# Order of the first loads, clears and splits, identity products ahead of the first keys, and key differences formed behind the first lower half, in a gated mix of two attentions

## The chip, the core and the metric

The kernel runs on one core of one Trainium2 chip. A core has five engines that work in parallel, each on its own list of instructions in a fixed order: TensorE (PE in the profile, with its weight loads as PEld) for matrix products into PSUM, VectorE (DVE), ScalarE (ACT), GpSimd (POOL), and SyncE (SP), which here only starts DMA transfers. ACT and POOL start transfers too. An engine waits for another through semaphores; the instruction that waits holds up all that stands behind it on its engine. The metric is the device time of one execution in microseconds (us), lower is better; each time is the median of several runs, and one further execution of each kernel is profiled.

## The reference

Two attentions read the same x (2048 rows of 512), and a gate mixes their outputs. Branch A is a local attention of 32 heads over 8 keys, two rows apart; branch B has 32 query heads and one head of keys and values, over all 2048 keys.

```python
def _A_ref(x, wqkv, wo):                      # H = 32, Dh = 16, W = 8, dil = 2
    q, k, v = qkv[0], qkv[1], qkv[2]          # of x @ wqkv
    idx = pos[:, None] - off[None, :]         # off = arange(8) * 2
    logits = einsum("bhsd,bhswd->bhsw", q, k[idx]) * scale
    attn = softmax(where(idx >= 0, logits, -1e9))
    return einsum("bhsw,bhswd->bhsd", attn, v[idx]) @ wo

def _B_ref(x, wq, wk, wv, wo):
    q = (x @ wq), 32 heads of 16;  k = x @ wk;  v = x @ wv
    p = softmax(einsum("bhqd,bkd->bhqk", q, k) * Dh ** -0.5)
    return einsum("bhqk,bkd->bhqd", p, v) @ wo

g = sigmoid((x * gate_w).sum(-1))
return g * a + (1 - g) * b
```

## The kernel before, in words

The program has four stages. All numbers of lines are those of the profile before.

**Opening.** x arrives transposed in four blocks t of 512 rows, each in four pieces c of 128 x 512 (`xraw[t, c]`, 256 KB each); `wkr` holds the key weights, `wqr[0..3]` the raw query weights (256 KB each). SP starts the sixteen x pieces (L114), ACT `wkr` (L150) and the four query weights (L117). A value is carried as a high and a low part: ACT rounds the high part (L81), DVE or POOL subtracts it to get the low part (L82); this is `split`, with `split_x` for x and `split_wq` for the query weights. PE forms the keys of block t from `xraw` and `wkr` (`keys(t)`, L189, four products over 128 rows); ACT and DVE write them into `kst` (L193, L194). `first_query(m)` forms the queries of the first row block for column groups 0 and 1 (L826, twelve products); they go out to a scratch tensor `qd` (L206), and `stack(u)` reads them back as the stacked tile `qst` of unit u (L283, L284). Rows 32 to 63 and 96 to 127 of each `qst` tile are cleared once (`clear`, L159), the halo of branch A's scratch tensor `ad` is written with zeros (L819, L820), the right half of `vst` with ones (L821).

**Front stream** (`front_stream`). PE runs the remaining query products and branch A's projections (L1002). These 78 lumps of twelve steps are split over the two halves of the PE array: the lower half takes the first 64 rows of the contraction, the upper half the last 64, and both add into one PSUM bank, so that a lower and an upper product can run at the same time. Between them stand products of queries with keys (L315) whose maxima DVE takes (L349): these are the running maxima that softmax needs for each unit. A cheaper form takes two key blocks at once: `kd` holds differences of keys, formed by `half_keys` (four products with `sel`, L365, over the full 128 rows) and `half_parts` (ACT L373, DVE L377); then a product with `kd` (L386), a relu on ACT (L396), a product with the keys (L315) and one DVE instruction (L406) give the maximum over two blocks. `queries_post` empties the PSUM bank of a finished query lump with two ACT copies (`qraw`, L217, of which there is a single buffer, and `qhi`, L218); POOL subtracts `qlo` (L225) from them, and SP writes both out.

**Exponentials.** For 512 steps PE forms scores (L454), ACT exponentials (L456), PE weighted sums (L465), with the remaining maxima (L315, L337, L349) and the output rows (L709) between them, while POOL works through branch A. **Tail**: the last four output rows.

What sets the order: the host code keeps three clocks (`clk`, for PE, ACT and DVE), one time for each PSUM bank at which it is expected to be free (`free`), and lists of tasks with due times. `front_stream` walks two positions, one per half of the array, and at each point writes down the step that its clocks say is ready. The clocks choose the order only; on the chip the engines follow that order at their own pace. The upper half may start a lump only behind a step of ACT or DVE that the plan expects to be finished (`behind`, `after_upper`). `wanted` says that the key differences are still to be formed: before, `half_keys` is written down as soon as both `pd` banks are expected to be free (29.0 on the plan's clocks, with the stream started at 26.5).

Of the kernel before, what the change touches and what calls it, by code (L numbers as in the profile page):

```python
# [6 lines left out]
F32 = mybir.dt.float32  # L7
# [41 lines left out]
def gated_mix_kernel(ctx, tc, xt, wa, wk, wq, wo_a, wo_b, out):  # L49
# [36 lines left out]
    def after(eng, ready, dur):  # L86
        clk[eng] = max(clk[eng], ready) + dur
        return clk[eng]
# [23 lines left out]
    def load_x(t):  # L112
        for c in range(C):
            nc.sync.dma_start(xraw[t, c], xt[:, t, c, :])  # L114

    def load_wq(cc):
        nc.scalar.dma_start(wqr[cc], wq[:, cc])  # L117
# [5 lines left out]
    def split_x(t, eng):  # L123
        for c in range(C):
            split(xh[t][c // 2][:, c % 2, :], xl[:, t, c, :], xraw[t, c], eng)
# [25 lines left out]
    for cc in range(4):  # L151
        load_wq(cc)
    for t in range(NQB):
        load_x(t)
    make_identity(nc, ident)

    def clear(k, eng):
        for b in (0, 64):
            eng.memset(qst[k][b + 32:b + 64].bitcast(F32), 0.0)  # L159

    for k in range(3):
        clear(k, nc.vector)

# [127 lines left out]
    free = {"m1": 0.0, "e0": 0.0, "e1": 0.0, "po": 0.0, "d0": 29.0, "d1": 29.0}  # L291
# [66 lines left out]
    wanted = [0]  # L358

    def half_keys():  # L360

        clk["pe"] = max(clk["pe"], free["d0"], free["d1"])
        for y in range(2):
            for g in range(2):
                nc.tensor.matmul(ds[g], sel[:, y], kst[:, (2 * g + y) * 512:(2 * g + y + 1) * 512], start=(y == 0), stop=(y == 1))  # L365
        clk["pe"] += 1.0
        free["d0"] = free["d1"] = clk["pe"] + 4.0
        tasks.append((clk["pe"] + 0.3, half_parts, (ups[0],)))

    def half_parts(up):  # L370
        kd.append(cp.tile([P, 2, 512], F32R, name="kd", tag="kd", bufs=1))
        for g in range(2):
            got = nc.scalar.activation(kd[0][:, g], ds[g], AF.Identity, scale=mk[:, 0:1])  # L373
            at = after("act", clk["pe"], 0.65)
            mark(got, at, up)
        for g in range(2):
            nc.vector.scalar_tensor_tensor(kd[0][:, g], ds[g], mk[:, 1:2], kd[0][:, g].bitcast(F32), op0=ALU.mult, op1=ALU.add)  # L377
            free[f"d{g}"] = after("dve", at + 0.1, 0.7) + 0.1
            formed.add(g)

# [434 lines left out]
    split_wq(0)  # L815
    for k in range(3, NB):
        clear(k, nc.gpsimd)
    zero = wp.tile([NAG, HALO * AN], F32, name="zero", tag="aext", bufs=2)
    nc.gpsimd.memset(zero, 0.0)  # L819
    nc.gpsimd.dma_start(ad[:, 0:HALO, :].rearrange("g r n -> g (r n)"), zero)  # L820
    nc.gpsimd.memset(vst[:, :, 16:32], 1.0)  # L821
# [24 lines left out]
    split_x(0, nc.vector)  # L846
# [8 lines left out]
    post_k()  # L855
    post_k = keys(2)
    post_q = first_query(1, fb[2])
    post_k()
    post_q()
# [6 lines left out]
    clk.update(pe=26.5, act=26.5, dve=26.5)  # L866
    stacked[:] = [0.0] * 2 + [30.0] * 2
    post_k()
    fill_one(m1, "m1")
    fill_one(po, "po")  # L870
    split_x(3, nc.gpsimd)
# [186 lines left out]
    def pick(b):  # L1058
# [11 lines left out]
        if not (ended and any(todo)) and (mine or slots and fillable() and not (paired() and not ended) and len(half) < 8) and (b or told[0] or mine):  # L1070
            for dst, key in ((m2[:, 0, :], "m2"),) if eb else zip(ds, ("d0", "d1")) if ended else ((m1, "m1"), (po, "po")):
                if fits(key):
                    return lambda dst=dst, key=key: fill_odd(b, dst, key)
# [4 lines left out]
    def front_stream(seq):  # L1078
# [4 lines left out]
        while told[0] < len(seq):  # L1083
            if wanted and max(free["d0"], free["d1"]) <= max(cl) + 0.05:
                wanted.clear()
                half_keys()
                cl = [clk["pe"]] * 2
                continue
# [172 lines left out]
```

## Time and profile before

| what | value |
|---|---|
| median of three runs | 1503.94 us (1502.19 to 1504.04) |
| the profiled execution | 1504.74 us, of which the span from first to last instruction is 1503.0 us |
| PE, DVE, ACT, POOL busy | 1481.7, 1198.1, 1251.3, 944.5 us |
| mean granted TensorE clock | 0.997 of full speed |
| first product of the keys | 5.29 us |
| first product of the front stream | 27.79 us |
| first lump products on both halves at once | 37.76 us |

A busy PE says only that some product was running. A product that covers 64 of the 128 rows leaves the other half of the array free, and two such products can overlap; a row such as "0.95 PE ... x2" is such a pair. The two stages to look at are the opening and the first 15 us of the front stream; the rest of the kernel runs on after them in an order that the same plan makes.

### The profile page before, as it was taken

To read this page: it belongs to the slowest core of one execution; us is meant where nothing else is said; L and a number is where in the kernel's file an instruction comes from. 1 tells how busy PE (TensorE), PEld (TensorE's weight loads), DVE (VectorE), ACT (ScalarE), POOL (GpSimd) and SP (SyncE) were. 2 spreads that over 40 slices of the span, in tenths; PEclk is the share of its full clock that TensorE was granted. 3 is DMA by queue.
4 is the path that set the end of the run, shared out by engine and by line. 5 is a ranking of instruction groups with operands and counts; after the bars stand their busy time and mean duration, and the time that the engine had idled before them with its cause. 6 is when DMAs were issued, how large, how long until landed. Compare 5 with 4: busy or idle time off the path is not lost.

```text
span 1503.0 us, 29096 instructions
## 1 busy us (share of the span) xinstructions
PE 1481.7 (99%) x10945; PEld 730.0 (49%) x10945; DVE 1198.1 (80%) x1789; ACT 1251.3 (83%) x1591; POOL 944.5 (63%) x1667
## 2 busy tenths in 40 slices
PE   8999999999999999999999999999999999999998
PEld 4899999633333333333333373333333733373334
DVE  5777878778888888888888888888888888888821
ACT  4787988699999999999999939999999489939994
POOL 7331898887979888888889787887840401151000
PEclk9999999999999999999999999999999999999999
DMA  6553342320211210211202111121100000000000
GB/s 219 144 162 114 116 144 80 97 77 12 77 51 38 86 38 31 77 48 41 77 13 69 45 59 46 41 69 41 41 12 12 23 19 2 1 23 8 1 2 29
DMA packets 43909, 85.64 MB, mean 57 GB/s; under 512 B 9520, under 2 KB 25960, under 8 KB 39672
## 3 DMA queue, kind: packets, MB, share of 16 engines
q1 hardware_dynamic: 36200, 44.00, 9.7%
q0 software_dynamic: 6560, 37.95, 7.8%
q8 instruction: 86, 1.41, 0.4%
q10 hardware_dynamic: 1008, 1.84, 0.3%
q14 instruction: 55, 0.45, 0.1%
HBM read 57.97 MB, written 25.25 MB: 55 GB/s over the span
## 4 chain that ended last, share of the span: by engine, by line
PE 93%; DVE 3%; ACT 1%; issue 1%; DMA 1%; DVEq 0%; ACTq 0%
PE po L465 32%; PE pe L454 25%; PE pf L1002 11%; PE pm L315 8%; PE ps L315 5%; PE pe L709 5%; PE pd L386 2%; DVE mx L337 1%; PE po L315 1%; PE pf L189 1%; DVE mx L349 1%; DVE tt L479 1%; PE pe L1192 1%; DMA ad<-stage 0%; ACT pexp L456 0%
## 5 line engine op out<-in xcount | busy, mean ns | idle before, releaser
L456 ACT ACTIVATE pexp<-pe 128x1024 f32<-128x1024 f32 x1024 | 991.1, 1022 | 94.3 <-PE pe L454 91.5
L337 DVE TENSOR_REDUCE mx<-pm 128x2 f32<-128x1024 f32 x525 | 641.0, 1221 | 165.7 <-PE pm L315 158.0
L454 PE MATMUL pe<-qst,kst 64*128 64x512 f32 x2048 | 566.9, 455 | 2.6 <-ACT pexp L456 1.2
L465 PE MATMUL po<-pexp,vst 128*32 128x512 f32 x4096 | 545.5, 605 | 3.4 <-DVE tt L479 2.3
L454 PEld LDWEIGHTS pe<-qst,kst 64*128 64x128 f32 x2048 | 233.7, 184 | 450.4 <-ACT pexp L456 442.2
L349 DVE TENSOR_REDUCE mx<-ps 128x1 f32<-128x512 f32 x476 | 323.9, 681 | 8.3 <-PE ps L315 7.3
L315 PE MATMUL ps<-kst,qst 62*128 62x512 f32 x602 | 252.4, 419 | 1.1 <-DVE mx L349 1.1
L315 PE MATMUL pm<-kst,qst 62*128 62x512 f32 x1054 | 222.7, 404 | 0.8 <-DVE mx L337 0.6
L527 POOL TENSOR_TENSOR pr<-aext 128x256 f32<-128x256 f32 x256 | 181.8, 737 | 4.8 <-PE pd L386 4.6
L587 POOL TENSOR_TENSOR oa<-oa,av 128x256 f32<-128x256 f32 x224 | 164.0, 732 | 15.7
L396 ACT ACTIVATE dd<-pd 128x512 f32<-128x512 f32 x252 | 147.6, 603 | 30.7 <-DVE mx L406 16.5
L465 PEld LDWEIGHTS po<-pexp,vst 128*32 128x32 f32 x4096 | 80.6, 108 | 179.8 <-issue 166.1
L315 PEld LDWEIGHTS ps<-kst,qst 62*128 62x128 f32 x602 | 111.2, 185 | 78.9 <-DVE mx L349 74.4
L584 POOL TENSOR_TENSOR av<-aext,lg 128x256 f32<-128x256 f32 x224 | 139.2, 622 | 13.6
L491 POOL TENSOR_TENSOR rl<-rl,gate_t 128x16 f32<-128x16 f32 x31 | 6.9, 221 | 190.5 <-DVE rl L485 190.4
L1002 PE MATMUL pf<-wah,xl 64*128 64x384 f32 (+1 forms) x496 | 121.1, 339 | 0.0
L1002 PE MATMUL pf<-wal,xh 64*128 64x384 f32 (+1 forms) x496 | 118.8, 338 | 0.0
L1002 PE MATMUL pf<-wah,xh 64*128 64x384 f32 (+1 forms) x496 | 117.2, 338 | 0.0
L406 DVE CUSTOM_DVE_ANT_0 dd<-po,dd 128x512 f32<-128x512 f32 x126 | 87.0, 691 | 31.8 <-PE po L315 17.8
L315 PEld LDWEIGHTS pm<-kst,qst 62*128 62x128 f32 x1054 | 103.4, 187 | 11.8 <-DVE mx L337 8.8
L406 DVE CUSTOM_DVE_ANT_0 dd<-ps,dd 128x512 f32<-128x512 f32 x126 | 87.0, 690 | 19.4 <-PE ps L315 5.6
L386 PE MATMUL pd<-kd,qst 62*128 62x512 f32 x252 | 100.8, 405 | 1.1 <-ACT dd L396 1.0
(188 smaller groups left out, 1610.6 us busy)
## 6 DMA issues: line engine op xcount, KB each, us to landing
aext<-ad POOLq DMA_DIRECT2D x32, 1056.0 KB, 5.6
ad<-stage SPq DMA_DIRECT2D x32, 384.0 KB
qst<-qd SPq DMA_DIRECT2D x64, 128.0 KB
xraw<-xt SPq DMA_DIRECT2D x16, 256.0 KB
qd<-qhi SPq DMA_DIRECT2D x16, 256.0 KB
qd<-qlo SPq DMA_DIRECT2D x16, 256.0 KB
qst<-qd SPq DMA_DIRECT2D x64, 64.0 KB
qst<-ml SPq DMA_DIRECT2D x228, 2.0 KB
```

Of the source, the lines that this page charges most:

```text
L315: nc.tensor.matmul(dst, qst[place(v)][b:b + 62, pr, t * P:(t + 1) * P], kst[b:b + 62, kc * 512:(kc + 1) * 512], start=True, stop=True)
L337: got = nc.vector.tensor_reduce(m[:, :, pr, t, kc], dst, AX.X, ALU.max)
L349: got = nc.vector.tensor_reduce(m[:, odd, pr, t, kc:kc + 1], dst, AX.X, ALU.max)
L396: got = nc.scalar.activation(dd[:, b], ds[b], AF.Relu)
L406: got = nc.vector.tensor_tensor_reduce(dd[:, b], dst, dd[:, b], 1.0, -FMAX, ALU.add, ALU.max, m[:, b, pr, t, kc:kc + 1])
L454: nc.tensor.matmul(bank[:, odd, :], kst[b:b + 64, kt * P:(kt + 1) * P], qst[place(u)][b:b + 64, pr, :], start=True, stop=True)
L456: got = nc.scalar.activation(e, bank, AF.Exp, scale=SCALE)
L465: nc.tensor.matmul(po[32 * i:32 * i + 32, :], vst[:, kt, :], pexp[s, i // 2][:, i % 2, :], start=(kt == 0), stop=(kt == NJ - 1))
L527: nc.gpsimd.tensor_mul(pr[:, k], q, e[:, o:o + NH, AC:2 * AC])
L584: nc.gpsimd.tensor_mul(av, e[:, o:o + NH, 2 * AC:].rearrange("p j (h d) -> p j h d", d=DH), lg[:, w].unsqueeze(3).to_broadcast([P, NH, AG, ...
L587: nc.gpsimd.tensor_add(ao, ao, av)
L1002: inst = nc.tensor.matmul(home(x)[0][:, :n], l[h], r[h], start=(i == 0 and b == 0), stop=(i == 3 * C - 1 and b == 1))
```

## The change

The diff touches the opening and the plan of the front stream.

- **Loads.** `wq` pieces 1 to 3 move from ACT's queue to SP's, each behind the x block of the same number; ACT starts `wkr` and `wq` piece 0 alone.
- **Clears.** DVE no longer clears three `qst` tiles first. POOL clears tiles 0 and 1 and writes the ones of `vst`; DVE clears tiles 2 and 3 between the posts of the keys; POOL clears tiles 4 to 8 as tasks of the front stream. The zeros of `ad` are written behind the third x block's low parts. The splits of the fourth x block are tasks too, one per piece.
- **Splits.** x piece 0 is split ahead of the first query weights.
- **Identity products.** Ten products of `ident` with itself (128 x 128, F32) stand ahead of the first keys; nothing reads what they write.
- **Last keys.** The first two products for maxima are written down ahead of the post of the last keys, so their DVE instructions stand ahead of it.
- **Key differences.** `half_keys` waits until the lower half has done the twelve steps of its first lump; the two ACT steps follow it at once, and the two DVE steps come when the plan's clock has passed them.
- **Plan.** The stream's clocks start at 24.6 in place of 26.5, the `pd` banks at 24.0 in place of 29.0; a half product for a maximum is taken by the lower half only once the upper half has done a step.

```diff
     def load_wq(cc):
-        nc.scalar.dma_start(wqr[cc], wq[:, cc])
+        (nc.sync if cc else nc.scalar).dma_start(wqr[cc], wq[:, cc])
...
-    def split_x(t, eng):
-        for c in range(C):
+    def split_x(t, eng, cs=range(C)):
+        for c in cs:
             split(xh[t][c // 2][:, c % 2, :], xl[:, t, c, :], xraw[t, c], eng)
...
     nc.scalar.dma_start(wkr, wk)
-    for cc in range(4):
-        load_wq(cc)
+    load_wq(0)
     for t in range(NQB):
         load_x(t)
+        if t:
+            load_wq(t)
     make_identity(nc, ident)
+    for k in range(10):
+        nc.tensor.matmul(m1[:, 0:P], ident, ident, start=True, stop=True)
...
-    for k in range(3):
-        clear(k, nc.vector)
-
+    for k in range(2):
+        clear(k, nc.gpsimd)
+    nc.gpsimd.memset(vst[:, :, 16:32], 1.0)
...
-    free = {"m1": 0.0, "e0": 0.0, "e1": 0.0, "po": 0.0, "d0": 29.0, "d1": 29.0}
+    free = {"m1": 0.0, "e0": 0.0, "e1": 0.0, "po": 0.0, "d0": 24.0, "d1": 24.0}
...
-    wanted = [0]
+    wanted = [0.0]
 
     def half_keys():
 
-        clk["pe"] = max(clk["pe"], free["d0"], free["d1"])
         for y in range(2):
             for g in range(2):
                 nc.tensor.matmul(ds[g], sel[:, y], kst[:, (2 * g + y) * 512:(2 * g + y + 1) * 512], start=(y == 0), stop=(y == 1))
         clk["pe"] += 1.0
-        free["d0"] = free["d1"] = clk["pe"] + 4.0
-        tasks.append((clk["pe"] + 0.3, half_parts, (ups[0],)))
-
-    def half_parts(up):
         kd.append(cp.tile([P, 2, 512], F32R, name="kd", tag="kd", bufs=1))
         for g in range(2):
             got = nc.scalar.activation(kd[0][:, g], ds[g], AF.Identity, scale=mk[:, 0:1])
-            at = after("act", clk["pe"], 0.65)
-            mark(got, at, up)
+            mark(got, after("act", clk["pe"] + T_LAT, 0.65))
+            free[f"d{g}"] = clk["act"] + 5.0
+        wanted[:] = [clk["act"] - 0.6]
+
+    def half_parts():
         for g in range(2):
             nc.vector.scalar_tensor_tensor(kd[0][:, g], ds[g], mk[:, 1:2], kd[0][:, g].bitcast(F32), op0=ALU.mult, op1=ALU.add)
-            free[f"d{g}"] = after("dve", at + 0.1, 0.7) + 0.1
+            free[f"d{g}"] = after("dve", free[f"d{g}"] - 5.0, 0.7) + 0.1
             formed.add(g)
+        wanted.clear()
...
     lumps = []
-    split_wq(0)
-    for k in range(3, NB):
-        clear(k, nc.gpsimd)
-    zero = wp.tile([NAG, HALO * AN], F32, name="zero", tag="aext", bufs=2)
-    nc.gpsimd.memset(zero, 0.0)
-    nc.gpsimd.dma_start(ad[:, 0:HALO, :].rearrange("g r n -> g (r n)"), zero)
-    nc.gpsimd.memset(vst[:, :, 16:32], 1.0)
...
-    split_x(0, nc.vector)
+    split_x(0, nc.vector, [0])
+    split_wq(0)
+    split_x(0, nc.vector, range(1, C))
     post_k()
...
     post_k()
+    clear(2, nc.vector)
     post_k = keys(2)
     post_q = first_query(1, fb[2])
     post_k()
+    clear(3, nc.vector)
     post_q()
...
     post_k = keys(3)
-    clk.update(pe=26.5, act=26.5, dve=26.5)
+    clk.update(pe=24.6, act=24.6, dve=24.6)
     stacked[:] = [0.0] * 2 + [30.0] * 2
-    post_k()
     fill_one(m1, "m1")
     fill_one(po, "po")
-    split_x(3, nc.gpsimd)
+    post_k()
+    for e in ("act", "dve"):
+        after(e, 0, 0.8)
+    zero = wp.tile([NAG, HALO * AN], F32, name="zero", tag="aext", bufs=2)
+    nc.gpsimd.memset(zero, 0.0)
+    nc.gpsimd.dma_start(ad[:, 0:HALO, :].rearrange("g r n -> g (r n)"), zero)
+    for c in range(C):
+        tasks.append((29.0 + 1.5 * c, split_x, (3, nc.gpsimd, [c])))
+    for k in range(4, NB):
+        tasks.append((37.0 + 3.5 * (k - 4), clear, (k, nc.gpsimd)))
...
-        if not (ended and any(todo)) and (mine or slots and fillable() and not (paired() and not ended) and len(half) < 8) and (b or told[0] or mine):
+        if not (ended and any(todo)) and (mine or slots and fillable() and not (paired() and not ended) and len(half) < 8) and (b or told[0]):
...
-            if wanted and max(free["d0"], free["d1"]) <= max(cl) + 0.05:
-                wanted.clear()
-                half_keys()
-                cl = [clk["pe"]] * 2
+            if wanted and wanted[0] <= max(cl) and at[0] >= 3 * C:
+                clk["pe"] = max(cl)
+                if kd:
+                    half_parts()
+                else:
+                    half_keys()
+                    cl = [clk["pe"]] * 2
                 continue
```

Three places show how the instructions move. A number behind a name tells one buffer of a pool from another.

On PE, the first rows of the front stream, from the seventh lower product on (`pf_97` is the bank of the first lump; `ps` and `po` take products for maxima; `pd` the key differences). Before:

```order
L1002 MATMUL pf_97<-xh,wqh 128x512
L1002 MATMUL pf_97<-xl,wqh 128x512
L365 MATMUL pd_92<-kst,sel 128x512
L365 MATMUL pd_93<-kst,sel 128x512
L365 MATMUL pd_92<-kst,sel 128x512
L365 MATMUL pd_93<-kst,sel 128x512
L1002 MATMUL pf_97<-xh,wql 128x512
L315 MATMUL ps<-kst,qst_76 128x512
```

And in the change, from the same point:

```order
L1009 MATMUL pf_97<-xh,wqh 128x512
L318 MATMUL po<-kst,qst_76 128x512
L1009 MATMUL pf_97<-xl,wqh 128x512
L1009 MATMUL pf_97<-xh,wql 128x512
L1009 MATMUL pf_97<-xh,wqh 128x512
L1009 MATMUL pf_97<-xl,wqh 128x512
L1009 MATMUL pf_97<-xh,wql 128x512
L367 MATMUL pd_92<-kst,sel 128x512
L367 MATMUL pd_93<-kst,sel 128x512
L367 MATMUL pd_92<-kst,sel 128x512
L367 MATMUL pd_93<-kst,sel 128x512
L1009 MATMUL pf_98<-xh,wqh 128x512
```

The four full products now stand behind all twelve lower products of the first lump; before they stood behind eight. Behind them come, in the change, five lower products of the second lump and two products for maxima, then the first upper product; before, eleven lower products and five for maxima stood between them and the upper half's first product.

On DVE, around the post of the last keys (`kst<-pf_98`). Before:

```order
L82 TENSOR_TENSOR qlo<-pf_99,qhi 128x512
L82 TENSOR_TENSOR wql<-dd,wqh 128x4x128 x2
L194 SCALAR_TENSOR_TENSOR kst<-pf_98,mk,kst 128x512
L349 TENSOR_REDUCE mx<-ps 128x1
L349 TENSOR_REDUCE mx<-po 128x1
```

And in the change:

```order
L162 MEMSET qst_79 32x1024 x2
L82 TENSOR_TENSOR qlo<-pf_99,qhi 128x512
L82 TENSOR_TENSOR wql<-dd,wqh 128x4x128 x2
L352 TENSOR_REDUCE mx<-ps 128x1
L352 TENSOR_REDUCE mx<-po 128x1
L197 SCALAR_TENSOR_TENSOR kst<-pf_98,mk,kst 128x512
```

The two maxima moved ahead of the keys' last step, and a clear stands further ahead.

On POOL, from the low parts of x on (`xh_119` and `xh_120` belong to the fourth x block). Before:

```order
L82 TENSOR_TENSOR xl<-xraw,xh 128x512 x8
L82 TENSOR_TENSOR xl<-xraw,xh_119 128x512 x2
L82 TENSOR_TENSOR xl<-xraw,xh_120 128x512 x2
L225 TENSOR_TENSOR qlo<-qraw,qhi 128x512 x2
L130 DMA waraw<-wa 128x402
```

And in the change:

```order
L82 TENSOR_TENSOR xl<-xraw,xh 128x512 x8
L873 MEMSET zero 16x1344
L874 DMA ad<-zero 16x1344
L82 TENSOR_TENSOR xl<-xraw,xh_119 128x512 x2
L82 TENSOR_TENSOR xl<-xraw,xh_120 128x512 x2
L228 TENSOR_TENSOR qlo<-qraw,qhi 128x512
L162 MEMSET qst_80 32x1024 x2
L228 TENSOR_TENSOR qlo<-qraw,qhi 128x512
L162 MEMSET qst_81 32x1024 x2
L130 DMA waraw<-wa 128x402
```

The zeros moved behind the third x block's low parts, and a pair of clears stands behind each of the first five `qlo`.

## The prediction

> **What bounds the kernel now.** I read the page first.
>
> ```profile
> span 1503.0 us, 29096 instructions
> ...
> PE 1481.7 (99%) x10945; PEld 730.0 (49%) x10945; DVE 1198.1 (80%) x1789; ACT 1251.3 (83%) x1591; POOL 944.5 (63%) x1667
> ...
> PE 93%; DVE 3%; ACT 1%; issue 1%; DMA 1%; DVEq 0%; ACTq 0%
> ```
>
> PE is busy nearly throughout and holds 93% of the chain of waits: PE time saved early moves the rest forward, if PE stays the bound behind it. So I asked for the stages, with PE and the granted clock (PEclk).
>
> ```profile
> 5.29:11.40 6.11, 6.11 (x9) 2.43 (x9) 5.48 (x20) 2.82 (x5) 5.85 (x8) 1.00 0.99 325
> ...
> 28.39:31.81 3.42, 2.35 (x11) 1.17 (x9) 2.94 (x5) 2.77 (x6) 3.42 (x3) 1.00 0.39 117
> 31.81:35.22 3.41, 3.41 (x10) 2.27 (x10) 0.89 (x2) 1.26 (x2) 3.41 (x4) 0.50 0.38 115
> 35.22:38.63 3.41, 3.41 (x14) 2.81 (x13) 2.01 (x4) 0.00 (x0) 1.59 (x2) 0.50 0.02 5
> 38.63:42.05 3.42, 3.42 (x20) 3.12 (x18) 2.24 (x5) 0.00 (x0) 0.00 (x0) 0.50 0.00 0
> 42.05:45.46 3.41, 3.41 (x28) 3.05 (x26) 1.79 (x4) 2.04 (x4) 0.88 (x1) 1.00 0.00 0
> ...
> 60.00:277.57 217.57, 216.44 (x2181) 209.06 (x2179) 170.20 (x508) 180.57 (x394) 139.82 (x251) 1.00 0.44 132
> ...
> 284.39:287.80 3.41, 2.48 (x17) 1.02 (x17) 1.38 (x2) 2.82 (x5) 3.33 (x13) 1.00 0.37 115
> 289.20:1490.00 1200.80, 1192.78 (x8417) 471.01 (x8416) 984.18 (x1196) 1030.01 (x1129) 757.99 (x1355) 1.00 0.12 37
> ```
>
> Two stages stand out. From 31.81 to 42.05 the granted clock is 0.50, and 10.24 x 0.5 / 1503 is all that the whole execution's mean clock lacks: there is no other such spell. It follows a stretch with PE busy 2.35 of 3.42 us on 11 products. And PE's count says more than its busy time: the products of the front stream cover half the array.
>
> ```profile
> core 0: 1503.0 us, clock 0.997
> ...
> 27.79:42.05 14.26, 13.19 (x50) 0.64 0.23 69
> 45.46:60.00 14.54, 14.54 (x127) 1.00 0.59 148
> ```
>
> In the steady stream a half product costs 14.54/127 = 0.1145 us (pairs overlap). From 27.79 to 42.05 PE ran 50, four of them full ones that count twice: 54 x 0.1145 = 6.2 us of steady work in 14.26 us. **8.1 us are lost there**: 5.1 by the clock (10.24 us at half speed), the rest by a gap and by an upper half that stands empty. The gap:
>
> ```profile
> 27.79 0.50 PE L315 MATMUL ps<-kst,qst 62*128 62x512 f32 x1
> ...
> 30.27 0.50 PE L315 MATMUL ps<-kst,qst 62*128 62x512 f32 x1 [1.07 <-DVE mx L349]
> ...
> 31.76 2.06 PE L365 MATMUL pd<-kst,sel 128*128 128x512 f32 x4
> ...
> 37.76 0.95 PE L1002 MATMUL pf<-xh,wqh 64*128 64x512 f32 x2
> ```
>
> The third product for a maximum waits at 30.27 for the first one's maximum; the upper half's lumps begin only at 37.76. What made that maximum late is the order on DVE and ACT:
>
> ```profile
> 28.74 0.34 ACT L307 ACTIVATE mx<-ident,mk 128x64 f32<-128x64 f32 x1
> ...
> 28.87 0.75 DVE L194 SCALAR_TENSOR_TENSOR kst<-pf,mk,kst 128x512 fp32r<-128x512 f32 x1 [1.89 <-ACT kst L193]
> 29.54 0.68 DVE L349 TENSOR_REDUCE mx<-ps 128x1 f32<-128x512 f32 x1
> ```
>
> The product ended by 28.3, but DVE first finished the last keys. The other stage is the opening:
>
> ```profile
> 5.29 6.24 PE L189 MATMUL pf<-xraw,wkr 128*128 128x512 f32 x7 [5.29 <-DMA wkr<-wk]
> ...
> 8.84 0.34 PEld L189 LDWEIGHTS pf<-xraw,wkr 128*128 128x128 f32 x1 [0.34 <-issue]
> 9.75 0.29 PEld L189 LDWEIGHTS pf<-xraw,wkr 128*128 128x128 f32 x1 [0.57 <-DMA xraw<-xt]
> 10.55 0.34 PEld L189 LDWEIGHTS pf<-xraw,wkr 128*128 128x128 f32 x1 [0.51 <-issue]
> ...
> 11.40 0.80 PE L826 MATMUL po<-xh,wqh 128*128 128x512 f32 x1
> ...
> 14.60 6.60 PE L189 MATMUL pf<-xraw,wkr 128*128 128x512 f32 x15
> ```
>
> Each key product is two instructions with a weight load each. In the first block they come (10.55 - 8.84)/2 = 0.85 us apart; later 15 of them take 6.60, 0.43 apart with the last one's tail taken off. So the first block runs at half clock too, whatever the 1.00 of its stage says. The fourth x piece is in by 9.75.
>
> **The change part by part**, against the profiled execution's 1504.74 us.
>
> *Opening.* By 9.75 nine transfers of 256 KB shared the DMA engines (`wkr`, four weights, four x pieces); now three weights stand behind. 0.79 MB at the 325 GB/s of 5.29:11.40 is 2.4 us, so the fourth piece lands between 7.35 and, if it gains little, 8.9; I take 8.2. Ten identity products issue twenty instructions of 128 columns. At half clock one takes a quarter of 0.85, 0.21 us, if its weight load hides, else up to the 0.34 of the load at 8.84. `ident` is there at 1.32:
>
> ```profile
> 1.03 0.29 POOL masks.py:199 TENSOR_SCALAR_AFFINE_SELECT ident<-ident 128x128 f32<-128x128 f32 x1
> ```
>
> From 1.4 on they end between 5.7 and 8.2; I take 5.7, as the key products hide their loads. They cost no time up to 5.29, when the first keys could start, and buy an earlier full clock: it came 6.1 us after the first product in the opening, 4.3 us after the first pairs later (37.76 to 42.05). Counted from 1.4, that is 5.7 to 7.5. With eight key instructions from 5.7, at 0.85 until then and 0.43 behind, held by the fourth piece at 8.2, the keys end between 9.1 and 10.4, against 11.40. **-1.5 us**, with ends -2.3 and +1.1 (identity products that don't raise the clock: 5.7 + 8 x 0.85 = 12.5).
>
> The Trainium skill, "TensorE: Matmul & The Clock Gate", section "What's actually happening", has the clock rise after a busy window of about 3.4 us that runs free of the program. By it the full clock would come from 4.8 to 8.2 and the keys end at 9.1 to 10.4 as well; the trace's spell of 10.24 us is three such windows, so it agrees.
>
> Behind it PE is unbroken to 27.79, so the gain reaches the stream, unless the first `qst` tile is late:
>
> ```profile
> 20.34 0.60 SPq L283 DMA_DIRECT2D qst<-qd  x1
> ...
> 22.23 0.57 SPq L284 DMA_DIRECT2D qst<-qd  x1
> ...
> waraw<-wa POOLq DMA_DIRECT2D x2, 201.0 KB, 3.2
> ...
> ad<-zero POOLq DMA_DIRECT2D x1, 84.0 KB, 4.9
> ```
>
> Those reads follow writes that queue behind all loads, whose bytes are unchanged; so they stay at 20.34. Issued at 22.23, the last of four lands 3.2 (`waraw`'s median) to 4.9 us later, 25.4 to 27.1; the stream now wants it at 26.3. At worst this takes back 0.8.
>
> *Stream.* The maxima move ahead of the keys' step: the third product then waits for ACT's `mx`, now ahead of the keys too, and one DVE maximum (0.68), some 0.1 us. Up to the upper half's first lump product, PE runs 18 lower products, 5 upper ones beside them and 4 full ones (the order of the change): 22 slots of 2 x 0.1145, 5.0 us, with 0.25 for that wait and the first product's start. Its steady work is (18 + 8 + 5) x 0.1145 = 3.55, so 1.75 us are lost in place of 8.1 if the clock stays: **-6.3 us**. Does it stay? Where it fell, 10 half products and a full one stood in 28.39:31.81. The new start has 3.41/0.229 = 15 lower products in such a stretch and two or three upper ones, about 17; 284.39:287.80 with 17 kept full clock. So it should.
>
> *POOL.* Five of nine clears now stand behind the stream's start, with the zeros and the fourth block's low parts ahead of the first `qlo`.
>
> ```profile
> 1.18 0.91 DVE L159 MEMSET qst<- 32x1024 f32 x1 [0.27 <-issue]
> ...
> 1.38 11.78 POOL L159 MEMSET qst<- 32x1024 f32 x12
> 13.19 1.21 POOL L819 MEMSET zero<- 16x1344 f32 x1
> ...
> 26.69 10.12 POOL L82 TENSOR_TENSOR xl<-xraw,xh 128x512 fp32r<-128x512 f32 x8 [5.16 <-ACT xh L81]
> ...
> 53.93 1.29 POOL L225 TENSOR_TENSOR qlo<-qraw,qhi 128x512 fp32r<-128x512 f32 x1 [1.88 <-issue]
> 57.03 1.29 POOL L225 TENSOR_TENSOR qlo<-qraw,qhi 128x512 fp32r<-128x512 f32 x1 [1.82 <-ACT qhi L218]
> ```
>
> A tile's clear is 2 x 11.78/12 = 1.96 us, and POOL idles 1.82 to 1.88 ahead of a `qlo`: it just fills the idle. The first `qlo` comes behind zeros (1.21 and its issue) and four low parts (5.1). `qraw` has one buffer, so ACT waits there for POOL's last `qlo`, and the relus behind it, for which PE waits, are late. From nothing (relus have slack) to 1.4 us at the first lump and 0.5 at four others, 3.4; I take **+1.2**, nearer nothing since PE runs ahead.
>
> *Maxima.* 519 stand ahead of the first scores, 524 before: 5 x 0.1145 less there; later five more pairs and five fewer single products, equal slots. **-0.3** (0 to -0.6). DVE's six early clears (0.91 each) lay beside the loads, its four later ones do beside unbroken key products: nothing. SP's three added loads stand behind x pieces needed sooner: nothing.
>
> Sum: -1.5 - 6.3 + 1.2 - 0.3 = -6.9; 1504.74 - 6.9 = **1497.8 us**. The profiled execution lies 0.8 above the median shown; I keep its base, as its spell's length may differ between executions.
>
> **The rivals.**
>
> *The slow clock stays* (0.12). The lower half still runs alone for most of a lump, and the limit lies somewhere between 11 and 17 products. Three stretches at half clock take 5.1 back: 1502.9; two, 1501.2. Against it: 284.39:287.80. The Trainium skill, "TensorE: Matmul & The Clock Gate", section "Why this matters for your kernels", warns only of PE gaps over about 3 us. By it a gap of 1.07 us did not lower the clock, closing it would not help, and this rival's time follows; the trace has the clock fall behind that gap.
>
> *The opening gains nothing* (0.10): loads stay DMA-bound, or identity products delay the keys as much as they speed them. 1497.8 + 1.5 = 1499.3. For it: DMA share 0.99 there; against: five transfers, not eight, precede the fourth piece beside it.
>
> *The later order gets worse* (0.08, slower). The plan's clocks differ, so most later rows stand elsewhere; where a maximum on DVE comes late PE waits. From 289.20 PE idles 1200.80 - 1192.78 = 8.0 us. It decides from 6.9 us more, where the gain is gone, and the kernel is slower from 9.9; at two and a half times today's idle, +12, 1509.8. Against it: equal slots, and output rows stand behind the same numbers of exponentials but for the last four.
>
> **How the numbers follow.** The forecast has 0.70. Its ends: -2.3 - 6.6 + 0 - 0.6 = -9.5, 1495.2, and with 3.4 for POOL and the late tile 1500.8. I take 1494.8 to 1502.0, which holds nearly all of it, the second rival and part of the first. 0.2%, 3.0 us, is what a measurement can tell: faster means under 1500.9. Forecast and second rival nearly all: 0.77; same, mostly the first rival: 0.15; slower 0.08.
>
> **What would show it.** In the changed profile: first queries (L821) near 9.9; the stream's first product by 26.5; clock 1.00 from there on; the first maximum ahead of the last `kst` on DVE; pairs on both halves some 5.5 us behind the stream's start; the first exponentials 6 to 8 us sooner, and that lead kept to the end. It is wrong if a spell at 0.50 stands behind 28 us, if ACT waits for POOL at `qraw` over 1 us a lump, or if PE's idle behind the front grows by the lead.

## The result, and the profile after

The changed kernel takes 1496.67 us (median of 5 runs, 1496.10 to 1497.07) against 1503.94 (1502.19 to 1504.95, 5 runs) for the kernel before on the same chip: a ratio of 0.9953, 95% interval 0.9938 to 0.9967. The profiled execution took 1497.07. The forecast was 1497.8.

In the later comparisons the runs of the kernel before fall into two groups, told apart by the mean granted clock: in 54 of 109 runs it was 0.999 or more, in 55 it was 0.998 or less. On the chip of the first of those comparisons the medians of the two groups are 1499.43 (20 runs) and 1504.44 (15 runs); the 5.0 us between them are nearly the 5.1 that 10.24 us at half clock cost. So, by the clocks, the spell at 0.50 that the prediction found in the profile is in about half of the executions. By their times, all five runs of the kernel before in the comparison above are of the group with the spell; all runs of the changed kernel have 0.999 or more. A mean of 0.999 leaves room for one window of 3.41 us at half clock, so "without the spell" below means at most one such window.

The page of the changed kernel, with the span, the busy times and the chain of waits:

```profile
span 1495.3 us, 29133 instructions
...
PE 1479.2 (99%) x10965; PEld 728.3 (49%) x10965; DVE 1199.4 (80%) x1783; ACT 1251.0 (84%) x1589; POOL 946.8 (63%) x1669
...
PE 92%; DVE 4%; issue 1%; ACT 1%; POOL 1%; DMA 1%; SPq 0%; DVEq 0%; ACTq 0%; POOLq 0%
```

PE is the bound as before. PE's timeline in the changed kernel (start, duration, engine, line, operation, idle time and what ended it) at the opening and at the stream's start:

```profile
1.37 4.64 PE L158 MATMUL ps<-ident 128*128 128x128 f32 x20 [1.37 <-POOL ident masks.py:199]
5.80 4.21 PE L192 MATMUL pf<-xraw,wkr 128*128 128x512 f32 x8
9.45 0.80 PE L821 MATMUL po<-xh,wqh 128*128 128x512 f32 x1
...
25.83 0.49 PE L318 MATMUL ps<-kst,qst 62*128 62x512 f32 x1
...
27.28 0.50 PE L318 MATMUL ps<-kst,qst 62*128 62x512 f32 x1
...
29.35 1.21 PE L367 MATMUL pd<-kst,sel 128*128 128x512 f32 x4
...
31.10 0.58 PE L1009 MATMUL pf<-xh,wqh 64*128 64x512 f32 x2
```

The first queries start at 9.45 in place of 11.40, the stream at 25.83 in place of 27.79; the third product for a maximum waits so little that no idle time is put down to it (1.07 before), and the first pair on both halves comes 5.27 us behind the stream's start, where it took 9.97. The windows of the changed kernel (length, then busy time and count of PE, PEld, DVE, ACT and POOL, the granted clock, DMA share and GB/s) show what stands where the clock fell before:

```profile
27.50:30.91 3.41, 3.41 (x18) 2.24 (x17) 2.18 (x4) 0.55 (x1) 3.41 (x4) 1.00 0.32 100
```

Eighteen products, four of them full ones, in place of eleven; no window at 0.50 stands behind the opening. DVE has the order that the diff writes:

```profile
26.55 0.68 DVE L352 TENSOR_REDUCE mx<-ps 128x1 f32<-128x512 f32 x1
27.15 0.67 DVE L352 TENSOR_REDUCE mx<-po 128x1 f32<-128x512 f32 x1
27.75 0.73 DVE L197 SCALAR_TENSOR_TENSOR kst<-pf,mk,kst 128x512 fp32r<-128x512 f32 x1
```

The gain is kept to the end, as the exponentials' row of the view by tile says (count, shortest, median and longest duration in ns, first and last start). Before:

```profile
L456 ACT ACTIVATE pexp<-pe x1024: 1016/1023/1052, 279.2 to 1478.3; 128x1024 f32<-128x1024 f32 x171
```

and in the changed kernel:

```profile
L458 ACT ACTIVATE pexp<-pe x1024: 1017/1023/1049, 271.2 to 1470.6; 128x1024 f32<-128x1024 f32 x171
```

The lead is 8.0 us at the first exponential and 7.7 at the last; between the second profiles of both kernels (277.9 and 270.8 at the first exponential) it is 7.1. At the first `qraw` it had been 8.85, as ACT's timeline of the kernel before

```profile
43.42 0.60 ACT L217 ACTIVATE qraw<-pf 128x512 f32<-128x512 f32 x1 [8.72 <-PE pf L1002]
```

and of the changed kernel show:

```profile
34.57 0.60 ACT L220 ACTIVATE qraw<-pf 128x512 f32<-128x512 f32 x1 [1.39 <-PE pf L1009]
39.31 0.60 ACT L220 ACTIVATE qraw<-pf 128x512 f32<-128x512 f32 x1 [1.36 <-POOL qlo L228]
...
87.58 0.60 ACT L220 ACTIVATE qraw<-pf 128x512 f32<-128x512 f32 x1 [1.11 <-POOL qlo L228]
```

Between these places the lead moves (6.1 us at the first `stage` copy, which starts at 96.87 before and 90.75 after), and about one us is lost on the way. The last two rows, where ACT waits for POOL at the single `qraw` buffer, are where the experiments look for it.

### The profile page after: what moved, and what is told of

It is laid out like the page before. It is cut to its first block, busy times and chain, and to the rows that moved or that the text cites. A ratio compares the mean times of both kernels' runs of the same rounds, so it can differ in the third digit from the quotient of the medians.

```text
span 1495.3 us, 29133 instructions
## 1 busy us (share of the span) xinstructions
PE 1479.2 (99%) x10965; PEld 728.3 (49%) x10965; DVE 1199.4 (80%) x1783; ACT 1251.0 (84%) x1589; POOL 946.8 (63%) x1669
## 3 DMA queue, kind: packets, MB, share of 16 engines
q10 hardware_dynamic: 576, 1.05, 0.2%
## 4 chain that ended last, share of the span: by engine, by line
PE 92%; DVE 4%; issue 1%; ACT 1%; POOL 1%; DMA 1%; SPq 0%; DVEq 0%; ACTq 0%; POOLq 0%
PE po L467 33%; PE pe L456 25%; PE pf L1009 10%; PE pm L318 9%; PE ps L318 5%; PE pe L711 4%; PE pd L388 2%; DVE mx L340 2%; PE po L318 1%; DVE tt L481 1%; DVE mx L352 1%; PE pe L1202 1%; POOL xl L82 1%; ACT qst L639 0%; DMA qd<-qhi 0%
## 5 line engine op out<-in xcount | busy, mean ns | idle before, releaser
L352 DVE TENSOR_REDUCE mx<-ps 128x1 f32<-128x512 f32 x471 | 320.5, 680 | 5.8 <-PE ps L318 5.8
L318 PE MATMUL ps<-kst,qst 62*128 62x512 f32 x596 | 248.5, 417 | 0.0
L1009 PE MATMUL pf<-wah,xl 64*128 64x384 f32 (+1 forms) x496 | 116.3, 338 | 0.0
L1009 PE MATMUL pf<-wah,xh 64*128 64x384 f32 (+1 forms) x496 | 113.7, 338 | 0.0
```

The costliest lines, as they stand in the source:

```text
L318: nc.tensor.matmul(dst, qst[place(v)][b:b + 62, pr, t * P:(t + 1) * P], kst[b:b + 62, kc * 512:(kc + 1) * 512], start=True, stop=True)
L352: got = nc.vector.tensor_reduce(m[:, odd, pr, t, kc:kc + 1], dst, AX.X, ALU.max)
L1009: inst = nc.tensor.matmul(home(x)[0][:, :n], l[h], r[h], start=(i == 0 and b == 0), stop=(i == 3 * C - 1 and b == 1))
```

## The experiments

The theory was the prediction's: the stream's start loses time by the clock and by an upper half that stands empty, the opening adds some 1.5 us, POOL takes a little back. Ten variants and the two kernels once more tested its parts. Within one comparison all runs share a chip; where different chips are set beside each other, the kernel before's own groups are the yardstick ("without" and "with" the spell, by the mean clock).

**The opening alone.** The kernel before with the change's loads, identity products, split order and clears (all of these ahead of the stream), its own stream order:

```diff
+        (nc.sync if cc else nc.scalar).dma_start(wqr[cc], wq[:, cc])
+    for k in range(10):
+        nc.tensor.matmul(m1[:, 0:P], ident, ident, start=True, stop=True)
+    split_x(0, nc.vector, [0])
+    split_wq(0)
+    split_x(0, nc.vector, range(1, C))
```

> The changed opening (loads, clears, splits, identity products; the late clears and the zeros put where POOL idles ahead of the stream) with the front stream of before. My theory: opening and stream add up. The stream starts 2.0 us sooner, the gap of 1.1 us and the spell at half clock stay, so -1.5 to -2.3 us: 1501.6 to 1502.4. Rival (the opening holds the clock up): no spell, -5.5 to -7, 1497 to 1498.5.

Measured: 1501.96 (12 runs), ratio 0.9999 [0.9987, 1.0011], in two groups: five runs at 1498.09 to 1499.30 with a clock of 0.999 or more, seven at 1501.81 to 1502.65 with 0.996 or 0.997. By group it is 0.9 (1498.55 against 1499.43) and 2.0 us (1502.43 against 1504.44) under the kernel before; the overall ratio says nothing, since it mixes the groups. The opening does not keep the clock up. The profiled execution is one of the five (1498.88, clock 0.999), and even it lost one window:

```profile
26.00:29.41 3.41, 2.34 (x10) 1.16 (x10) 3.11 (x6) 2.62 (x6) 3.41 (x3) 1.00 0.56 183
29.41:32.83 3.42, 3.42 (x10) 2.28 (x10) 1.04 (x3) 1.26 (x2) 3.42 (x4) 0.50 0.42 121
```

**The stream alone.** The changed kernel with the kernel before's loads, clears and splits and without identity products:

```diff
-    load_wq(0)
+    for cc in range(4):
+        load_wq(cc)
-    for k in range(10):
-        nc.tensor.matmul(m1[:, 0:P], ident, ident, start=True, stop=True)
+    split_x(0, nc.vector)
```

> The opening of before (loads on ACT's queue, clears and zeros first, no identity products) with the changed order of the front stream. My theory: the stream starts at 27.8 as before, no spell, no gap over 0.3 us, and no late clears behind qlo: -5.5 to -6.5 us, 1497.4 to 1498.4. Rival (the opening holds the clock up): the spell is back, -1 to -2, 1502 to 1503.

Measured: 1497.19 (1496.67 to 1497.93, 11 runs), one group, clock 0.999 or more in all; ratio 0.9975 [0.9964, 0.9985]. That is 2.2 us under the kernel before without the spell and 7.3 under it with the spell. The first queries start at 10.50 here, 1.05 later than in the changed kernel, and yet the first exponential starts at the same time:

```profile
L454 ACT ACTIVATE pexp<-pe x1024: 1017/1023/1049, 270.9 to 1470.2; 128x1024 f32<-128x1024 f32 x171
```

So the stream's order makes nearly all of the gain, and beside it the opening's lead does not reach the end.

**No identity products.** The changed kernel without its two lines for them.

> The changed kernel without the ten identity products. My theory: the first keys run at half clock up to about 10, the first queries start at 9.9 to 11 in place of 9.45, and all the rest moves by that: +0.5 to +1.5 us on the changed kernel, 1497.2 to 1498.2; the clock stays up in the stream. Rival (they only fill time in which PE would wait for the loads anyway): within 0.3 us of the changed kernel. Rival (the opening holds the clock up): the spell is back, +5.

Measured: 1497.27 (1496.31 to 1498.39, 12 runs), ratio 0.9972 [0.9961, 0.9982], clock 0.999 or more. PE's timeline:

```profile
4.86 5.19 PE L190 MATMUL pf<-xraw,wkr 128*128 128x512 f32 x8 [4.86 <-DMA wkr<-wk]
9.49 0.80 PE L819 MATMUL po<-xh,wqh 128*128 128x512 f32 x1
```

The keys could have started at 4.86; the identity products hold them until 5.80, and both kernels reach the first queries at the same time, 9.49 and 9.45. A second profile of the changed kernel had them at 8.73, so their worth lies between nothing and 0.8 us there. The expected delay to 9.9 or later did not come; at the end 0.3 to 0.6 us lie between this variant and the two medians of the changed kernel, which were taken on other chips, so the runs don't tell whether any is lost. In the start the first rival holds, not the theory.

**Keys ahead of the maxima.** The changed kernel with `post_k()` back in front of the first two maxima:

```diff
+    post_k()
     fill_one(m1, "m1")
     fill_one(po, "po")
-    post_k()
```

> The changed kernel with the last keys' post ahead of the first two products for maxima again, on ACT and DVE; PE's order is the same. The third product for a maximum then waits some 1.1 us, as it did before. If the clock falls for such a gap (gap theory): a spell at 0.50 of at least two stretches of 3.4 us, +4.5 to +6.2 on the changed kernel, 1501 to 1503. If it falls for how little of the array is filled (my theory): the stretch around the gap still holds about 14 half products, between the 11 at which it fell and the 17 at which it held, so +1.1 with the clock up is likelier than not, 1497.8; a spell in some executions only would set the limit near 14.

Measured: 1499.37 (1497.60 to 1500.60, 12 runs), ratio 0.9982 [0.9971, 0.9993]; in five runs the clock was 0.997 or 0.998. The wait is back, and the profiled execution kept its clock behind it, against the gap theory; PE's row, and the window around it, which holds 12 products, two of them full:

```profile
28.22 0.50 PE L318 MATMUL ps<-kst,qst 62*128 62x512 f32 x1 [1.07 <-DVE mx L352]
```

```profile
27.33:30.75 3.42, 2.53 (x12) 1.85 (x13) 2.72 (x5) 0.00 (x0) 3.42 (x4) 1.00 0.38 115
```

This one line of order is worth about 2.1 us (1499.37 less the 1497.27 of the variant above, on the same chip; that one also lacks the identity products). Part of it is that clock is lost again, since the five runs have a median of 1500.35 and the other seven of 1499.02. Where those five lost it is not known, as none was profiled. That some executions lose it and others keep it is what the expectation put down to a limit near 14 half products.

**The changed kernel and the kernel before, again.** No edit.

> The changed kernel once more, beside many runs of the kernel before. Theory: the kernel before loses the clock behind its first maxima only in some executions, and the changed kernel never: its runs lie in one group, 1496 to 1498, at a mean clock of 0.999 or more, and the ratio over many runs of before is 0.997 to 0.998, not the 0.9953 of the first comparison, whose five runs of before all had the spell. Rival: the gain is 7 us in every execution, and the ratio is 0.995 to 0.996 again.

> The kernel before, profiled once more. Theory: its runs fall into two groups, near 1499.5 with a mean clock of 1.000 and near 1504.2 with 0.997, about 5 us apart, which is what 10.24 us at half the clock take. If the profiled execution is one of the first group, its first exponentials come about 5 us sooner than 279.20. Rival: the two groups differ in something else than the spell, and a profiled execution at 1499 to 1500 has the spell too or lacks it without a gain at the first exponentials.

Measured: the changed kernel 1496.92 (1496.60 to 1497.26, 11 runs), ratio 0.9970 [0.9959, 0.9981], clock 0.999 or more in all; the kernel before 1503.67 (12 runs), five at 1498.71 to 1500.11 with a clock of 1.000 and seven at 1503.53 to 1505.17 with 0.996 or 0.997. Against the 34 runs of the kernel before beside them (19 without, median 1499.09; 15 with, 1503.72) the change gains 2.2 or 6.8 us. The theory of two groups holds. The profiled execution of the kernel before was one with the spell:

```profile
26.70:30.11 3.41, 2.34 (x11) 1.33 (x11) 2.18 (x4) 3.41 (x8) 3.41 (x4) 1.00 0.58 168
30.11:40.35 10.24, 10.24 (x33) 7.57 (x34) 4.67 (x8) 1.37 (x3) 5.77 (x5) 0.50 0.27 78
```

An execution of it without the spell was never profiled; what it looks like inside is inferred from the clocks alone.

**The kernel before with the gap filled.** Six products that nobody reads:

```diff
     fill_one(m1, "m1")
     fill_one(po, "po")
+    for k in range(6):
+        nc.tensor.matmul(fb[3], sel[:, 0], kst[:, 0:512], start=True, stop=True)
```

> The kernel before with six products of kst and sel into an unused PSUM bank right behind the first two maxima's products; nobody reads their result, and the order and the plan's clocks are the kernel before's. They take 6 x 0.233 = 1.4 us of PE, of which its wait of 1.07 for the first maximum goes. Theory (the clock falls where a window of 3.41 us is filled too little: the array was filled to 0.29 to 0.32 in the windows behind which it fell, to 0.41 or more where it stayed): the window's fill rises to about 0.65, no execution has the spell, all runs lie in one group at a mean clock of 0.999 or more, 1498.8 to 1500.3, 4 to 5 us under the slower group of the kernel before, though PE has more to do. Rival (the spell comes from the wait for the maximum, from the half-array products as such, or from something outside the start of the stream): two groups again, the slower near 1504.5.

Measured: a clock of 1.000 in eight runs and 0.999 in four, beside 10 of 17 runs of the kernel before at 0.998 or less. The window is full now:

```profile
26.54:29.95 3.41, 3.41 (x14) 1.86 (x13) 1.60 (x3) 3.41 (x8) 3.41 (x3) 1.00 0.69 207
```

This shows where the spell comes from: it hangs on the thin stretch behind the first maxima, since products added there alone, with the half-array products behind them left as they were, take it away. The six products fill PE's idle time and the array at once, so this run doesn't tell which of the two counts; the last section does. The price was missed: 1501.12 (1499.58 to 1504.26), ratio 0.9993 [0.9982, 1.0004], 1.5 us above the kernel before without the spell where up to 0.7 was expected. The four runs at 0.999 have a median of 1502.34, so some of the spread may be single windows at half clock; but the eight at 1.000 still have 1500.75, 1.2 above the six runs of the kernel before at 1.000 beside them (1499.57), and these runs don't explain that.

**Half keys early.** The changed kernel without the condition `at[0] >= 3 * C`; the four products for the key differences stand right behind the first two maxima. (What the expectation calls lumps of exponentials' columns are the twelve lower products of the first lump.)

> The changed kernel without the condition that the key differences be formed behind the first lower half's twelve lumps of exponentials' columns: their four products stand right behind the first two maxima, as before. Theory: those four products need the last kst, which DVE now writes behind the first maximum, so PE stops some 1.5 to 2.5 us there; three further maxima stand ahead of the first scores (0.3 us). 1498.5 to 1500.0 without a spell at half the clock, and since PE's gap returns, the spell returns in some executions (2 to 5 us more, mean clock 0.997 to 0.998). Rival: the position of the differences decides nothing, the time is within 0.5 of the changed kernel's and the clock stays at 0.999 or more in all.

Measured: 1505.64 (1501.39 to 1508.46, 12 runs), ratio 1.0028 [1.0015, 1.0041]; four runs at 0.999 or more have a median of 1504.04, the others 1507.3. Worse than either theory. The wait at the start is there, if a little shorter than expected; the fourth product for the key differences waits for `kst`. A larger one comes later. PE:

```profile
28.56 0.50 PE L367 MATMUL pd<-kst,sel 128*128 128x512 f32 x1 [1.31 <-DVE kst L197]
...
262.59 0.49 PE L388 MATMUL pd<-kd,qst 62*128 62x512 f32 x1 [2.85 <-ACT dd L398]
```

ACT ahead of it:

```profile
261.56 0.49 ACT L249 ACTIVATE stage<-pf 128x384 f32<-128x384 f32 x1 [3.51 <-DMA ad<-stage]
```

And the windows there:

```profile
259.67:263.09 3.42, 0.57 (x6) 0.46 (x6) 0.52 (x1) 1.47 (x3) 3.11 (x5) 1.00 0.57 193
263.09:266.50 3.41, 3.41 (x22) 3.41 (x22) 2.19 (x8) 2.29 (x4) 3.02 (x6) 0.50 0.00 0
```

ACT stands 3.51 us before a buffer whose store has not left, PE runs dry behind it, and the next window is at half clock. In all, PE's waits from 27 us to the first exponentials come to 6.7 us, where the changed kernel has 1.1, and the first exponentials start at 278.7, 7.5 us later. (The profiled execution is one of the four; the eight with a lower clock were not profiled.) This is the prediction's third rival, "the later order gets worse", which the change itself escaped: the plan's clocks reorder everything behind them.

**Clears where POOL idles.** The changed kernel with the later clears and the zeros moved:

```diff
     nc.gpsimd.memset(vst[:, :, 16:32], 1.0)
+    for k in range(4, 8):
+        clear(k, nc.gpsimd)
-    for k in range(4, NB):
-        tasks.append((37.0 + 3.5 * (k - 4), clear, (k, nc.gpsimd)))
```

> The changed kernel with the clears of tiles 4 to 7 right behind the writing of ones into vst, and the ninth clear and the zeros ahead of the stream's start, where POOL idles; the values are the same. Theory (POOL's added work costs time only where ACT waits for qlo ahead of the second lump's qraw, 1.36 us, and PE behind it for 0.53): that wait at qraw falls under 0.3 us, PE's with it, and the time is 0.3 to 0.8 less than the changed kernel's beside it. Rival: PE has other work at that place and the maxima fill it, so the time is within 0.2 of it. A second rival: the zeros' transfer and the clears now lie beside the loads and the first splits and delay the first queries from 9.45, at 0.5 to 1.5 us more.

Measured: 1496.96 (1496.20 to 1498.18, 12 runs), ratio 0.9974 [0.9964, 0.9985]: as the changed kernel beside it. The theory falls at its first step; the wait is there without the clears:

```profile
38.77 0.60 ACT L222 ACTIVATE qraw<-pf 128x512 f32<-128x512 f32 x1 [1.36 <-POOL qlo L230]
```

POOL's rows at that `qlo` say what it hung on, the fourth block's last low part, for which ACT had rounded `xh` late:

```profile
36.19 1.29 POOL L82 TENSOR_TENSOR xl<-xraw,xh 128x512 fp32r<-128x512 f32 x1 [0.70 <-ACT xh L81]
37.44 1.29 POOL L230 TENSOR_TENSOR qlo<-qraw,qhi 128x512 fp32r<-128x512 f32 x1
```

**A third `qlo` buffer, all three, and the splits alone.**

```diff
-    wkr = p0.tile([P, C, P], F32, name="wkr")
+    wkr = p0q.tile([P, C, P], F32, name="wkr", tag="qlo", bufs=3)
```

> The changed kernel with three buffers for qlo in place of two (wkr lies in the third until the last keys are done). Theory (part of the opening's gain is lost in the front where POOL's qlo waits for the transfers of earlier ones to qd, 3.3 us ahead of 86.25 in the changed kernel's profile, and ACT at qraw for POOL, 1.1 us at 87.58): that wait at the last qraw goes, the lead over the kernel before is kept from the first qraw to the first exponentials, and the time is 0.3 to 1.0 us less than the 1496.92 of the second comparison, 1496.0 to 1496.6. Rival: a later wait, for the stores of stage (1.0 us at 148.21 in the second profile of the changed kernel), takes the gain, and the time is within 0.2 of 1496.9.

```diff
-        tasks.append((29.0 + 1.5 * c, split_x, (3, nc.gpsimd, [c])))
+        tasks.append((25.5 + 0.5 * c, split_x, (3, nc.gpsimd, [c])))
```

> The third qlo buffer, the clears and zeros in POOL's idle time, and the fourth block's splits due at the plan's 25.5 to 27.0 in place of 29.0 to 33.5, so that ACT forms them ahead of kd and qraw, and POOL's low parts of it end ahead of the first qlo. Theory: ACT no longer waits for POOL ahead of the second lump's qraw (1.36 us), nor PE behind it (0.53), and with the wait at 87.58 gone too the time is 0.5 to 1.5 less than the changed kernel's, 1495.4 to 1496.4. Rival: the four splits, 2.2 us of ACT ahead of kd, delay the key differences and the pairs on them by up to 1 us and the time is 1496.7 to 1497.7.

> The changed kernel with only the due times of the fourth block's four splits altered, 25.5 to 27.0 in place of 29.0 to 33.5: on ACT the fourth one then stands ahead of the first lump's qraw; PE's order is the changed kernel's, the clears, the zeros and the two qlo buffers too. Theory (of the three edits of the combined kernel it is this one that pays, since the wait at the second lump's qraw hung on the fourth block's last low part and not on the clears): that wait falls from 1.36 to 0.7 or less, PE's 0.53 behind it goes, and the time is 1495.1 to 1496.0. Rival (it needs POOL free of clears as well, or the third buffer): 1496.5 to 1497.1, as the other variants of the changed kernel.

Measured: the buffer alone 1496.93 (1495.80 to 1497.76, 6 runs), no gain; all three 1495.17 (1494.61 to 1495.70, 6 runs, the same comparison), ratio 0.9950 [0.9936, 0.9964]; the splits alone 1496.04 (1495.50 to 1496.51, 6 runs, another chip), ratio 0.9956 [0.9942, 0.9970]. The last two lie just outside their ranges, the first of them below, the other 0.04 above. With the splits early, ACT waits at the second lump's `qraw` for PE, not for POOL, and PE's wait behind it is gone:

```profile
38.08 0.60 ACT L220 ACTIVATE qraw<-pf 128x512 f32<-128x512 f32 x1 [0.79 <-PE pd L388]
```

Measured against the group of the kernel before with the spell in each comparison, the changed kernel lies 6.8 us lower (1496.92 and 1503.72), the splits alone 8.2 (1496.04 and 1504.22), all three 8.8 (1495.17 and 1503.97). So the early splits are worth about 1.4 us and the combined kernel about 2.0; against the groups without the spell it is 1.9 and 2.2, with only three such runs beside the splits alone. The combined kernel beats both kernels. Whether the other two edits add to the splits is inside the scatter between chips.

The third buffer's rival came true. In that variant's own profile the last `qraw` no longer waits, and the wait for a store out of `stage` takes the lead:

```profile
85.95 0.59 ACT L220 ACTIVATE qraw<-pf 128x512 f32<-128x512 f32 x1
...
148.16 0.49 ACT L249 ACTIVATE stage<-pf 128x384 f32<-128x384 f32 x1 [1.09 <-DMA ad<-stage]
```

A second profile of the changed kernel, whose first queries were 0.72 us ahead of the first one's, has that wait too:

```profile
148.21 0.49 ACT L249 ACTIVATE stage<-pf 128x384 f32<-128x384 f32 x1 [1.04 <-DMA ad<-stage]
```

Work that arrives early waits for the transfer.

## Why the prediction was right, and where it was not

**The bound** held: PE has 92% of the chain, and time saved up to the first `qraw` came through but for one us.

**The opening** was put at -1.5 with ends of -2.3 and +1.1; the first queries moved by -1.95, and from execution to execution they move by almost one (10.44 in the second profile of the kernel before, 8.73 in that of the changed one). The first wrong step is "They cost no time up to 5.29, when the first keys could start": without the identity products the keys start at 4.86, and with them, since they end at 6.01 and not 5.7, at 5.80. "Behind it PE is unbroken to 27.79, so the gain reaches the stream" is right, but the stream passes it on only in part: the stream alone, which starts its first queries 1.05 us later, has its first exponential at the same time. The waits of `qraw` and `stage` on transfers are where it can go. Alone the opening is worth 0.9 to 2.0, beside the stream's order 0.3 to 0.5 (1497.19 less 1496.92 and 1496.67, medians from different chips). That `qst`'s reads stay at 20.34 was wrong by 0.5 us (19.86), at no cost.

**The stream** was put at -6.3. Up to the first pair 4.7 us less passed (9.97 less 5.27), and the lead grew from 1.96 at the stream's start to 8.85 at the first `qraw`, 6.9. Mechanism and sign are as forecast: the maximum ahead of the keys, no wait, no half clock. The step that failed is a sentence on the base: "I keep its base, as its spell's length may differ between executions". The spell does not differ only in length, it is absent from half of the executions; 5.1 of the 6.3 us are there only where it is present. The time came out because the changed kernel has no spell, so its own level does not depend on the base; the expected gain does. Against an execution without the spell it is 2.2 us, 0.15%, which the bound of 0.2% would have called no change. A median 0.8 below a profiled time did not show this; the runs beside each other with their clocks did. That the sum came out so near is in part luck: the stream alone, with ACT's wait of 1.4 us for POOL in it, gained 7.3 us where the spell is, more than was forecast for stream and POOL together, and the opening added at most 0.5 in place of 1.5.

**POOL** was put at +1.2, with up to "1.4 us at the first lump". ACT's wait is 1.36, at the second lump, and PE's behind it is small:

```profile
39.96 0.50 PE L1009 MATMUL pf<-xh,wqh 64*128 64x512 f32 x1 [0.53 <-ACT qraw L220]
```

Moving the splits gave back about 1.4 in all, by the groups. The size is right, the cause half right: of what the prediction named, the clears and the zeros moved away without effect, and the fourth block's low parts remain. What made the last of them late, its rounding on ACT, which the plan had put behind the first `qraw`, the prediction did not see. Its sign of being wrong, a wait of over 1 us at `qraw` for POOL, came at two of the fourteen lumps, not at each. The second wait, 1.11 at 87.58, is on a transfer:

```profile
86.25 1.29 POOL L228 TENSOR_TENSOR qlo<-qraw,qhi 128x512 fp32r<-128x512 f32 x1 [3.32 <-DMA qd<-qlo]
```

**Maxima** (-0.3) were not tried by themselves; no run tells them from the scatter.

**The rivals.** The slow clock did not stay: 17 or 18 products in a window kept it in the profiles, and no run of the changed kernel was under 0.999; the limit, put between 11 and 17 products, lies near 14 half products (last section). That the opening gains nothing is nearly true of its value at the end. The later order did not get worse in the change; one condition less, and it did.

## What to carry to other kernels

Ahead of a forecast, look at all runs of the kernel before with their clocks: a loss that the profile shows may be one that only some executions have, and then the gain has two sizes. At a start where few products stand between waits, the order of two instructions on the engine that frees PSUM can decide, in some of the executions, over the clock of the next 10 us. A lead won early ends where the work meets a store or a single buffer; ask for each which transfer it will wait for.

## What the runs showed of the hardware

The granted clock changed in steps of 3.41 us. How long PE is busy in such a window does not decide over it. The clock fell behind windows with 2.34 and 2.35 us busy, but in the variant with half keys early it stayed behind one with 1.90:

```profile
51.46:54.87 3.41, 1.90 (x17) 1.51 (x16) 1.41 (x5) 2.95 (x6) 3.23 (x5) 1.00 0.53 136
54.87:58.28 3.41, 3.41 (x33) 3.18 (x32) 2.61 (x8) 2.87 (x6) 3.24 (x5) 1.00 0.67 200
```

In the kernel before it stayed at 0.50 behind 31.81:35.22 and 35.22:38.63, although PE was busy throughout both. What goes with the clock in these traces is how much of the array the products fill. In the stream's windows, with a product over all 128 rows counted as two, it fell behind 6, 10 and 11 half products and stayed behind 14 (12 products, two of them full, in 2.53 us; 13 products, one of them full, in 2.42 us) and behind 17. Inside the spells it stayed low behind 10 to 14 and rose behind 14 or more. So the limit is near 14 half products in 3.41 us, by few windows and with products cut at their edges.

The Trainium skill, "TensorE: Matmul & The Clock Gate", section "Why this matters for your kernels", warns of PE gaps over about 3 us; here windows with one gap of 1.07 us were enough, in about half of the executions, and the window of 1.90 us above, with a gap of 1.51, was not. That the window's place against the program decides which executions have the spell is argued from where the windows lay, not shown.
